# Weight loads of a two-branch spectral filter: +k and -k rows from one DMA queue in turn, in place of two queues side by side

## The chip, the cores and the metric

The kernel runs on one core of one Trainium2 chip. The metric is the device time of one execution in microseconds (us). The core has five engines that work side by side, each with its own instruction queue: TensorE (PE; PEld is its weight load), VectorE (DVE), ScalarE (ACT), GpSimd (POOL) and SyncE (SP). SyncE and GpSimd only issue transfers here. "SPq" in the profile is an issue on SyncE's queue.

## The reference

Two branches, A and B, filter the same input in the frequency domain, and a gate mixes them. Branch B's function is the same as A's.

```python
def _A_ref(x, w_r, w_i):
    B, S, D = x.shape                       # 1, 2048, 1024, bfloat16
    X = rfft2(x.astype(float32), axes=(-2, -1))
    W = w_r + 1j * w_i                      # 2048 x 513 each, bfloat16
    return irfft2(X * W, s=(S, D), axes=(-2, -1)).astype(bfloat16)

x = A_x
g = sigmoid((x * gate_w).sum(-1, keepdims=True))
return g * _A_ref(x, A_w_r, A_w_i) + (1 - g) * _B_ref(x, B_w_r, B_w_i)
```

Only `A_x` is used; both branches share one forward transform.

## The kernel before

The transforms are written as matrix products. A row index of 2048 is split into 128 x 16, a column index is folded into even and odd halves, and constant matrices (FM, DM, S2, KI, DI, RM) carry the cosines and sines. All of x, the transformed x, and both weights lie in on-chip memory: R1 holds x, R4 the transform X, R5 the weight of A, R2 the weight of B. R1 is used again for the inverse result of A (`VR[0]`), and R5 for that of B (`VR[1]`). R2 also holds, before B's weight comes, the gate vector and a row of 2048 numbers made from it, under the keys `gwt` and `zrow`.

The work goes in stages.

1. For 16 slices of x: fold on VectorE (L316), then eight matmuls with FM (L313), then the eviction to R3 on ScalarE. Along the way `gate_row` makes the gate's spectral row, and 16 small matmuls turn it into ZG.
2. The main loop, t from 0 to 20. Step t issues `stage_d(t)` (matmuls with DM, evicted to the buffer Q), `stage_s2(t-1)` (matmuls with S2, evicted to R4 as X), `stage_i1(0, t-5)` (matmuls with KI on the products of A, evicted to R1 as V(0, k)), and at even t one `prod` on VectorE. `prod(b, m)` multiplies X(2m) and X(2m+1) by the weight of branch b: two large multiplications and two smaller combinations, all at L316. At t = 18 comes `prod(1, 0)`, at t = 20 `prod(1, 1)`. At t = 17 stand `x512`, `p512(0)` and `p512(1)`, which treat the last column, number 512, of both weights.
3. A second loop does `stage_i1(1, t)`, the remaining products of B, the gate's mixing rows (`gmix`, L566) and `stage_dinv(0, ...)` with DI.
4. A third loop does `stage_dinv(1, t)` and `s1inv(t-1)`, whose results go out in 16 transfers on SyncE's queue.

The order on each engine is the program's order; nothing is sorted. Class `Sched` works out the waits. Every operation names the keys that it reads and writes. An operation waits for the last writer of each key that it reads; for each key that it writes, it waits for the last writer and for all operations that have read the key since. A transfer counts as done when it has landed. `ev` (L302 on ScalarE, L304 on VectorE) picks the engine of an eviction by estimated loads of these two alone. Matmul results sit in three slots of PSUM in turn (`slot`).

The transfers are issued by `dma` (L319). SyncE's queue holds, in order: x in five pieces with FM behind the first, DM, S2, KI, GS, ID, then the rows of A from `wload(0)`, those of B from `wload(1)` (called at t = 0), DI, RM, two copies of one row (`v512_row`), and the outputs.

A weight's rows are laid out on the partitions so that a frequency k and its mirror -k can be used together. `wload(b)` loops over `ii` (four groups), `c` (real, imaginary) and `pm` (0 for +k rows, 1 for -k rows). Each piece is 16 partitions of 16 rows of 513 numbers, 1,026 bytes a row; the -k rows are read in falling order, and their last group is in two pieces. That makes 8 transfers of +k rows and 10 of -k rows, 4.2 MB for each weight. The +k rows are issued from SyncE, the -k rows from GpSimd. The GpSimd half names `("x", 15)`, the last piece of x, as read. Each half has a key of its own, `("W", b, 0)` and `("W", b, 1)`, and for B both also name `zrow` and `gwt` as written.

The eviction of V(0, 0), in `stage_i1`, is the first write into R1 after x; it names all 16 keys of x as written:

```python
w = [("V", b, kg)]
if kg == 0:
    w += allx if b == 0 else [("W", 0, 0), ("W", 0, 1)]
```

Of the kernel before, what the change touches and what calls it, by code (L numbers as in the profile page):

```python
# [234 lines left out]
def bass_gated_mix__spectral_gfnet__spectral_gfnet__prompt_kernel(  # L235
# [6 lines left out]
    def sb(name, n, dty=BF):  # L242
        t = nc.alloc_sbuf_tensor(name, [128, n], dty)
        pit[id(t)] = n
        return t

    def ap(t, off, dims, p0=0, np_=128):
        return AP(t, p0 * pit[id(t)] + off, [[pit[id(t)], np_]] + [list(d) for d in dims])
# [18 lines left out]
    X5 = sb("X5", 32)  # L267
# [19 lines left out]
    def slot():  # L287
        s = slot_n[0] % nslots[0]
        slot_n[0] += 1
        return s  # L290

    def dve(ns, fns, reads, writes):
        load["dve"] += ns
        return S.op("dve", fns, reads, writes)

    def ev(n, outap, inap, reads, writes, eng=None, bias=0.0):
        ca, cd = 170 + 0.833 * n, 150 + 1.04 * n
        if eng is None:
            eng = "act" if load["act"] + ca <= load["dve"] + cd + bias else "dve"
        load[eng] += ca if eng == "act" else cd  # L300
        if eng == "act":
            S.op("act", lambda e: e.activation(outap, inap, ACT.Copy), reads, writes)  # L302
        else:
            S.op("dve", lambda e: e.tensor_copy(outap, inap), reads, writes)  # L304

    def pslot(s, off, dims, p0=0, np_=128):
        return ap(PS, s * 1024 + off, dims, p0, np_)
# [4 lines left out]
    def mm(o, l, r, start, stop):  # L312
        return lambda e: e.matmul(o, l, r, start=start, stop=stop, skip_group_check=True)  # L313

    def tt(o, a, b, op):
        return lambda e: e.tensor_tensor(out=o, in0=a, in1=b, op=op)  # L316

    def dma(eng, pairs, reads, writes, kind=True):
        S.op(eng, [lambda e, d=d, s=s: e.dma_start(d, s) for d, s in pairs], reads, writes, dma=kind)  # L319
# [19 lines left out]

    def wload(b):  # L340

        both = ([], [])
        T = WR[b]
        P = pit[id(T)]
        for ii in range(4):
            for c in range(2):
                for pm in range(2):
                    src = wsrc[b][c]
                    n = src.shape[-1]
                    prs = both[pm]  # L350

                    def part(r0, step, k0, k1):
                        prs.append((AP(T, (4 * pm + ii) * P + (2 * k0 + c) * NS, [[8 * P, 16], [2 * NS, k1 - k0], [1, n]]),
                                    AP(src.tensor, src.offset + r0 * n, [[128 * n, 16], [step * n, k1 - k0], [1, n]])))
                    if pm == 0:
                        part(16 * ii, 1, 0, 16)
                    elif ii < 3:
                        part(80 + 16 * ii, -1, 0, 16)
                    else:
                        part(127, -1, 1, 16)  # L360
                        part(64, 1, 0, 1)
        dma("sp", both[0], [], [("W", b, 0)] + (["zrow", "gwt"] if b else []))
        dma("pool", both[1], [("x", 15)], [("W", b, 1)] + (["zrow", "gwt"] if b else []))
    wload(0)


# [44 lines left out]
    for n2 in range(16):  # L411
        w = ap(R2, n2 * 128, [[1, 128]], 0, 1)
# [6 lines left out]
    allx = [("x", m) for m in range(16)]  # L419
# [34 lines left out]
    def prod(b, m):  # L454

        T = WR[b]
        x = ap(R4, 2 * m * 1024, [[1024, 2], [512, 2], [1, 512]])
        w = ap(T, 2 * m * 2 * NS, [[2 * NS, 2], [NS, 2], [1, 512]])
        ws = ap(T, 2 * m * 2 * NS + NS, [[2 * NS, 2], [-NS, 2], [1, 512]])
        r = [("X", 2 * m), ("X", 2 * m + 1), ("W", b, 0), ("W", b, 1)]  # L460
        p = PO + m % 2 * 2048
        dve(1230, tt(ap(RING, TO, [[1024, 2], [512, 2], [1, 512]]), x, w, ALU.mult), r, ["t0"])
        dve(1230, tt(ap(RING, TO + 2048, [[1024, 2], [512, 2], [1, 512]]), x, ws, ALU.mult), r, ["t1"])
        for c, op in enumerate((ALU.subtract, ALU.add)):
            t = TO + 2048 * c
            dve(680, tt(ap(RING, p + c * 512, [[1024, 2], [1, 512]]), ap(RING, t, [[1024, 2], [1, 512]]),
                        ap(RING, t + 512, [[1024, 2], [1, 512]]), op), [f"t{c}"], [("P", m % 2, c)])
# [3 lines left out]
    def stage_i1(b, kg):  # L471
        s = slot()
        p = PO + kg // 2 % 2 * 2048 + kg % 2 * 1024
        z = 512 if kg == 0 else 0
        fns = []
        for lb in range(4):
            for c in range(2):
                w = ap(RING, p + c * 512 + lb % 2 * 256 + lb // 2, [[2, 128]])
                fns.append(mm(pslot(s, lb * 256, [[1, 256]]), w, ap(KI, z + c * 256, [[1, 256]]), c == 0, c == 1))
        S.op("pe", fns, [("P", kg // 2 % 2, 0), ("P", kg // 2 % 2, 1), "KI"], [("ps", s)])  # L480
        w = [("V", b, kg)]
        if kg == 0:
            w += allx if b == 0 else [("W", 0, 0), ("W", 0, 1)]
        ev(1024, ap(VR[b], kg * 8, [[128, 128], [1, 8]]), pslot(s, 0, [[8, 128], [1, 8]]), [("ps", s)], w)

    def x512():
# [2 lines left out]
    def p512(b):  # L489
        T, o = WR[b], b * 96  # L490
        x = ap(X5, 0, [[16, 2], [1, 16]])
        w = ap(T, 512, [[NS, 2], [2 * NS, 16]])
        ws = ap(T, NS + 512, [[-NS, 2], [2 * NS, 16]])
        r = ["X5", ("W", b, 0), ("W", b, 1)]
        dve(100, tt(ap(P5, o, [[16, 2], [1, 16]]), x, w, ALU.mult), r, [("p5", b, 0)])
        dve(100, tt(ap(P5, o + 32, [[16, 2], [1, 16]]), x, ws, ALU.mult), r, [("p5", b, 1)])
        for c, op in enumerate((ALU.subtract, ALU.add)):
            dve(100, tt(ap(P5, o + 64 + 16 * c, [[1, 16]]), ap(P5, o + 32 * c, [[1, 16]]),
                        ap(P5, o + 32 * c + 16, [[1, 16]]), op), [("p5", b, c)], [("P5", b, c)])
# [39 lines left out]
    for t in range(16 + 5):  # L539
        if t < 16:  # L540
            stage_d(t)
        if 1 <= t < 17:
            stage_s2(t - 1)
        if t >= 5:
            stage_i1(0, t - 5)
        if t >= 2 and t % 2 == 0:
            prod(t // 18, t // 2 - 1 - t // 18 * 8)
        if t == 0:
            wload(1)
            cload("sp", DI, "DI", 2048)  # L550
            cload("sp", RM, "RM", 2048)
        if t == 17:
            x512()
            p512(0)
            p512(1)
        if t == 19:
            v512(0)
            v512(1)
# [14 lines left out]
    for t in range(16 + LAG):  # L573
        if t < 16:
            stage_i1(1, t)
            if t % 2 == 1 and t // 2 + 2 < 8:
                prod(1, t // 2 + 2)
        if t in (8, 10, 12, 14):
            gmix((t - 8) // 2)
        if t == 15:  # L580
            v512_row(1)
        if t >= LAG:
            stage_dinv(0, t - LAG)
# [64 lines left out]
```

## Time and profile before

| What | Value |
|---|---|
| Median of 2 runs | 181.97 us (180.98 and 182.96) |
| Profiled execution, time | 182.96 us |
| Profiled execution, span of its instructions | 181.1 us |
| TensorE matmuls busy | 129.4 us (71%) |
| VectorE busy | 120.6 us (67%) |
| ScalarE busy | 121.6 us (67%) |
| GpSimd busy | 11.3 us (6%) |
| Bytes moved by DMA | 19.53 MB, mean 108 GB/s |

The profile is of one execution. The span runs from the first instruction to the last; the time of the execution is 1.86 us longer. "Busy" adds up the durations of an engine's instructions; a share of the span says nothing of where the idle time lies. Where lines stand in the text below, a group is named by its line in the kernel, its engine, the operation, and out<-in by the program's tile names without their numbers, so that R is any of R1 to R5.

### The profile page before, as it was taken

To read this page: it belongs to the slowest core of one execution; us is meant where nothing else is said; L and a number is where in the kernel's file an instruction comes from. 1 tells how busy PE (TensorE), PEld (TensorE's weight loads), DVE (VectorE), ACT (ScalarE), POOL (GpSimd) and SP (SyncE) were. 2 spreads that over 40 slices of the span, in tenths; PEclk is the share of its full clock that TensorE was granted. 3 is DMA by queue.
4 is the path that set the end of the run, shared out by engine and by line. 5 is a ranking of instruction groups with operands and counts; after the bars stand their busy time and mean duration, and the time that the engine had idled before them with its cause. 6 is when DMAs were issued, how large, how long until landed. Compare 5 with 4: busy or idle time off the path is not lost.

```text
span 181.1 us, 2542 instructions
## 1 busy us (share of the span) xinstructions
PE 129.4 (71%) x1015; PEld 91.9 (51%) x1024; DVE 120.6 (67%) x193; ACT 121.6 (67%) x132; POOL 11.3 (6%) x24
## 2 busy tenths in 40 slices
PE   0445998889600004999999559999699989998950
PEld 0345463555300003677776337889577757565620
DVE  0799990008950000268998999998693469899994
ACT  2255498399400005689889844899999959987970
POOL 0004700000009100000000000000000000000000
PEclk9999999999975555599999985999999999999997
DMA  6999999999998990000000000000000003334334
GB/s 180 331 423 374 171 224 222 218 165 166 166 243 169 161 144 0 0 5 2 0 0 4 0 0 0 5 0 0 4 0 0 1 4 116 116 138 157 121 114 171
DMA packets 10157, 19.53 MB, mean 108 GB/s; under 512 B 1505, under 2 KB 5793, under 8 KB 9762
## 3 DMA queue, kind: packets, MB, share of 16 engines
q1 hardware_dynamic: 8592, 15.17, 31.6%
q0 software_dynamic: 1408, 4.20, 12.3%
q8 instruction: 8, 0.13, 0.3%
q10 hardware_dynamic: 146, 0.00, 0.0%
q14 instruction: 3, 0.02, 0.0%
HBM read 15.17 MB, written 4.19 MB: 107 GB/s over the span
## 4 chain that ended last, share of the span: by engine, by line
ACT 31%; PE 27%; DMA 17%; DVE 13%; issue 5%; SPq 3%; POOL 2%; POOLq 0%; DVEq 0%; ACTq 0%
PE PS L313 27%; ACT R L302 20%; DMA R<-in_B_w_i_dram 14%; ACT RING L302 8%; DVE RING L316 7%; DMA R<-in_A_x_dram 4%; DVE R L316 3%; SPq L319 3%; DVE RING L304 3%; POOL R L319 2%; ACT GROW L566 1%; ACT L566 1%; ACT V L302 1%; POOLq L213 0%; DVEq L213 0%
## 5 line engine op out<-in xcount | busy, mean ns | idle before, releaser
L302 ACT ACTIVATE R<-PS 128x1024 bf16<-128x1024 f32 (+1 forms) x80 | 75.7, 1039 | 42.8 <-DMA R<-in_B_w_i_dram 22.0
L316 DVE TENSOR_TENSOR RING<-RING 128x512 bf16<-128x512 bf16 (+1 forms) x96 | 44.6, 509 | 22.5 <-PE PS L313 20.3
L316 DVE TENSOR_TENSOR RING<-R 128x2048 bf16<-128x2048 bf16 (+1 forms) x48 | 48.0, 1041 | 14.2 <-DMA R<-in_A_w_i_dram 6.8
L313 PE MATMUL PS<-KI,RING 128*128 128x256 bf16 x256 | 35.9, 291 | 26.4 <-ACT R L302 24.1
L302 ACT ACTIVATE RING<-PS 128x1024 bf16<-128x1024 f32 x40 | 42.8, 1135 | 8.5 <-PE PS L313 7.3
L313 PEld LDWEIGHTS PS<-KI,RING 128*128 128x128 bf16 x256 | 25.3, 104 | 33.7 <-ACT R L302 25.2
L313 PE MATMUL PS<-DI,R 128*128 128x256 bf16 x256 | 32.7, 273 | 1.5 <-DVE RING L304 1.2
L313 PEld LDWEIGHTS PS<-DI,R 128*128 128x128 bf16 x256 | 24.4, 98 | 8.4 <-DVE RING L304 2.2
L313 PE MATMUL PS<-FM,R 128*128 128x128 bf16 x128 | 12.0, 266 | 11.7 <-DVE R L316 11.4
L313 PE MATMUL PS<-RING,S 128*128 128x1 bf16 (+2 forms) x91 | 16.7, 315 | 1.3 <-ACT RING L302 0.8
L313 PE MATMUL PS<-DM,R 128*128 128x256 bf16 x128 | 17.3, 282 | 0.1
L313 PEld LDWEIGHTS PS<-FM,R 128*128 128x128 bf16 x128 | 10.1, 122 | 13.7 <-DVE R L316 12.3
L304 DVE CAST RING<-PS 128x1024 bf16<-128x1024 f32 x8 | 10.0, 1252 | 6.0 <-PE PS L313 6.0
L313 PEld LDWEIGHTS PS<-DM,R 128*128 128x128 bf16 x128 | 12.4, 101 | 2.9 <-ACT RING L302 0.7
L313 PEld LDWEIGHTS PS<-RING,S 128*128 128x128 bf16 x96 | 8.1, 100 | 8.1 <-ACT RING L302 1.4
L316 DVE TENSOR_TENSOR R<-RING 128x1024 bf16<-128x1024 bf16 x16 | 10.4, 688 | 0.3
L313 PE MATMUL PS<-R,FM 128*128 128x512 bf16 x30 | 9.1, 379 | 1.3 <-DVE RING L304 1.3
L313 PE MATMUL PS<-R,G 128*1 128x512 bf16 x32 | 8.8, 423 | 0.7 <-ACT R L302 0.7
L313 PE MATMUL PS<-RING,DM 128*128 128x512 bf16 x30 | 9.1, 379 | 0.1
L304 DVE CAST R<-PS 128x1024 bf16<-128x1024 f32 x4 | 4.9, 1223 | 3.1 <-PE PS L313 3.1
L313 PEld LDWEIGHTS PS<-R,G 128*1 128x1 bf16 x32 | 2.6, 90 | 5.8 <-issue 2.0
L313 PEld LDWEIGHTS PS<-RING,DM 128*128 128x128 bf16 x32 | 3.1, 98 | 3.8
(29 smaller groups left out, 36.0 us busy)
## 6 DMA issues: line engine op xcount, KB each, us to landing
out_dram<-RING SPq DMA_DIRECT2D x16, 256.0 KB, 2.0
R<-in_A_x_dram SPq DMA_DIRECT2D x3, 1024.0 KB, 10.5
R<-in_A_w_r_dram SPq DMA_DIRECT2D x4, 256.5 KB, 16.2
R<-in_A_w_i_dram SPq DMA_DIRECT2D x4, 256.5 KB, 17.8
R<-in_B_w_r_dram SPq DMA_DIRECT2D x4, 256.5 KB, 9.8
R<-in_B_w_i_dram SPq DMA_DIRECT2D x4, 256.5 KB, 10.8
R<-in_A_x_dram SPq DMA_DIRECT2D x2, 512.0 KB, 5.0
R<-in_A_w_r_dram POOLq DMA_DIRECT2D x3, 256.5 KB, 11.2
```

What stands on the lines that cost most here:

```text
L302: S.op("act", lambda e: e.activation(outap, inap, ACT.Copy), reads, writes)
L304: S.op("dve", lambda e: e.tensor_copy(outap, inap), reads, writes)
L313: return lambda e: e.matmul(o, l, r, start=start, stop=stop, skip_group_check=True)
L316: return lambda e: e.tensor_tensor(out=o, in0=a, in1=b, op=op)
L319: S.op(eng, [lambda e, d=d, s=s: e.dma_start(d, s) for d, s in pairs], reads, writes, dma=kind)
L566: S.op("act", lambda e: e.activation(ap(GROW, 0, [[1, 512]]), misc(7, 0, [[1, 512]]), ACT.Sigmoid), ["m7"], ["GROW"])
```

## The change

`wload` collects all pieces of a weight in one list, in the order of its loops: for each group and each of real and imaginary, the +k rows and then the -k rows. One `dma` on SyncE issues the list. It names nothing as read, and one key, `("W", b)`, as written (with `zrow` and `gwt` for B, as before). The users of the weight read that key. GpSimd issues no transfers any more. The order of instructions on TensorE, VectorE and ScalarE stays as it was.

```diff
     def wload(b):
 
-        both = ([], [])
+        prs = []
         T = WR[b]
         P = pit[id(T)]
         for ii in range(4):
...
                     src = wsrc[b][c]
                     n = src.shape[-1]
-                    prs = both[pm]
 
                     def part(r0, step, k0, k1):
...
-        dma("sp", both[0], [], [("W", b, 0)] + (["zrow", "gwt"] if b else []))
-        dma("pool", both[1], [("x", 15)], [("W", b, 1)] + (["zrow", "gwt"] if b else []))
+        dma("sp", prs, [], [("W", b)] + (["zrow", "gwt"] if b else []))
...
-        r = [("X", 2 * m), ("X", 2 * m + 1), ("W", b, 0), ("W", b, 1)]
+        r = [("X", 2 * m), ("X", 2 * m + 1), ("W", b)]
...
-            w += allx if b == 0 else [("W", 0, 0), ("W", 0, 1)]
+            w += allx if b == 0 else [("W", 0)]
...
-        r = ["X5", ("W", b, 0), ("W", b, 1)]
+        r = ["X5", ("W", b)]
```

## The prediction

> **What bounds the kernel now.** I read the waits first, then the timeline around the longest of them, then the transfer rates by stretch, and last the place where the second weight is first used. The table of waits has, per row, who waited on whom, the total in us, how often, and the longest.
>
> ```profile
> POOL R L319 <- DMA R<-in_B_w_i_dram: 32.5, 1, 32.5
> ...
> PE PS L313 <- ACT R L302: 26.0, 8, 22.0
> ACT R L302 <- DMA R<-in_B_w_i_dram: 22.0, 1, 22.0
> ...
> DVE RING L316 <- DMA R<-in_A_w_i_dram: 6.8, 1, 6.8
> ```
>
> One ScalarE instruction waits 22.0 us for the second weight's transfers, and TensorE's longest wait, 22.0 us, is for that instruction. Which one it is, the timeline tells (start, duration, engine, operation, and in brackets the idle time before it with its releaser):
>
> ```profile
> 41.36 2.36 DVE L316 TENSOR_TENSOR RING<-R 128x2048 bf16<-128x2048 bf16 x2 [6.80 <-DMA R<-in_A_w_i_dram]
> ...
> 45.22 1.03 PE L313 MATMUL PS<-KI,RING 128*128 128x256 bf16 x8
> 46.09 1.10 ACT L302 ACTIVATE R<-PS 128x1024 bf16<-128x1024 f32 x1
> ...
> 47.26 1.06 PE L313 MATMUL PS<-RING,S 128*128 128x512 bf16 x6
> ...
> 53.93 0.58 POOL L319 DMA_DIRECT2D R<-in_B_w_r_dram  x1 [32.47 <-DMA R<-in_B_w_i_dram]
> ...
> 69.20 1.02 ACT L302 ACTIVATE R<-PS 128x1024 bf16<-128x1024 f32 x1 [22.01 <-DMA R<-in_B_w_i_dram]
> ...
> 70.28 1.89 PE L313 MATMUL PS<-KI,RING 128*128 128x256 bf16 x8 [21.96 <-ACT R L302]
> ...
> 75.48 1.42 PE L313 MATMUL PS<-KI,RING 128*128 128x256 bf16 x8
> ```
>
> The matmuls at 45.22 are the first `stage_i1(0, 0)`; the activation at 69.20 is its eviction into R1. It does not use the second weight. It waits because it overwrites x (`allx`), and the GpSimd loads are entered as readers of `("x", 15)`: whoever overwrites x waits until both GpSimd loads have landed. The second of them was itself late. It and the SyncE half both list `zrow` and `gwt` as written, so GpSimd held its eight B issues until SyncE's half had landed at 53.65, and its own rows landed at 69.11. From 48.32 to 70.28 TensorE did nothing. It also came back at half clock: i1, d and s2 from 70.28 to 75.48 took 5.20 us, where three stages take about 3.15 elsewhere (1.03 to 1.06 each, as at 45.22 and 47.26); the granted clock in that stretch is 0.50, against 1.00 before the stall.
>
> **Part by part.** *Removed: the read of x15 and the second tile key.* There is now one load per weight, on SyncE, that reads nothing. The eviction of V(0,0) keeps only the wait for TensorE's matmuls. What it can then wait for is the first weight, through the product and i1(0,0).
>
> *Moved: ten issues per weight from GpSimd to SyncE.* Each takes about 0.61 us there (the B rows' issues at 34.98, 35.63 and on), so 6 us per weight. For A they fit where SyncE stood 15.8 us until 34.38, waiting for the gate's matmuls. If the queue holds SyncE back until room is free, the ten wait for 256 KB each at the rate below, 1.6 us, and the last leaves around 35 to 41, still before the queue runs dry. GpSimd's queue has nothing else in it. Behind the B rows on SyncE come DI, RM, the two `v512_row` copies and the outputs, in that order; none of them is wanted before 89 us on the new clock (below).
>
> *The price: one queue instead of two.* In these rows the last number is GB/s.
>
> ```profile
> 18.00:22.00 4.00, 4.00 (x20) 1.78 (x18) 3.93 (x7) 1.94 (x2) 3.47 (x7) 1.00 1.14 169
> 22.00:34.00 12.00, 10.27 (x98) 5.55 (x97) 5.36 (x9) 9.45 (x12) 0.00 (x0) 1.00 1.07 223
> ...
> 36.00:40.00 4.00, 3.25 (x27) 2.17 (x27) 0.00 (x0) 4.00 (x5) 0.00 (x0) 1.00 1.14 165
> ...
> 58.00:66.00 8.00, 0.00 (x0) 0.00 (x0) 0.00 (x0) 0.00 (x0) 1.42 (x3) 0.50 1.04 163
> ```
>
> SyncE's queue alone moves weight rows at 165 to 169 (36 to 40, and 18 to 22, when GpSimd's rows hardly flowed yet), GpSimd's alone 163 (58 to 66), both together 223. In the 8 us from 24 to 32 the two queues stood so (packets, MB, share of the 16 engines' time):
>
> ```profile
> q0 software_dynamic: 416, 1.37, 77.3%
> q1 hardware_dynamic: 417, 0.40, 28.0%
> ```
>
> GpSimd's queue took 171 GB/s, SyncE's only 50, which is why SyncE's last A load, issued at 17.89, landed 23.3 us later, at 41.2. [...]
>
> New landing of A: 4.20 MB at 165 GB/s is 25.5 us. The rate falls from 384 GB/s (16 to 17) over 289 to 173 (18 to 19), so weight rows begin at about 17.5: landed at 43.0. A second way to it: SyncE's half of B, 2.1 MB, followed A at 41.2 and landed at 53.65, so the slowest of the 16 engines needs 12.45 us per half, 24.9 for a whole; from 18 that gives 42.9. The first product starts at 43.0 instead of 41.36, ends 3.57 us later at 46.6, and i1(0,0) starts at 46.6 instead of 45.22: **+1.4 us**. (The product had 0.3 us to spare.) This rests on one thing no row shows: the -k rows, read in falling order, on SyncE's queue. The nearest rows are the same rows on GpSimd's queue (163) and the +k rows on SyncE's (165), so I take 165; the far bounds are 223 (both queues; A at 36.3, no loss) and 50 (SyncE's share beside GpSimd).
>
> *What follows.* i1(0,0) ends at 47.65; ScalarE, free since 47.19, evicts it at 47.7 instead of 69.20. TensorE runs d(6) and s2(5) to 49.8 and goes straight on with i1(0,1): its bank is free at 48.7. So the 21.96 us of idle time go: **-22.0**. The clock has no reason to fall in a gap of 1.4 us, so the next three stages take 3.15 instead of 5.20: **-2.05**. The following pair, i1(0,2) and d(8), took 2.34 to 77.82 and should take 2.1: **-0.2**. Sum: -22.8 us; the stage at 77.82 starts at 55.0.
>
> What could take it back behind that? VectorE worked ahead during the stall: it did the product at 49.88 while the others stood. Now product 1 runs 46.6 to 50.2, a cast to 51.4, product 2 to 55.0. Product 2 is wanted by i1(0,4), two rounds of 2.65 after i1(0,2) at 52.9, so at 58; cover 3 us. The cast of d(8) then begins at 55.0, and 77.81 less 22.8 is 55.0. The rounds from 77.82 on are TensorE's (5.3 us for two, VectorE 4.9), unchanged. That products don't slow down beside transfers is seen in their durations: 2.36 for the pair at 45.14, with the queues full, and 2.36 at 79.76, with none.
>
> *The wait that is added.* B's first user now waits for B itself; before, ScalarE's stall had covered it. It is the small product `p512(1)` on VectorE:
>
> ```profile
> 104.58 0.34 DVE L316 TENSOR_TENSOR P<-X,R 128x32 bf16<-128x32 bf16 x2
> ```
>
> Behind it VectorE has all products of B, and TensorE's i1(1, ...) waits for those. On the new clock it comes at 81.8. B follows A in the same queue: 43.0 + 25.5 = 68.5, so 13 us are to spare. DI and RM (1 MB; 254 GB/s from 50 to 54) land at 72.6; DI is wanted at 115.68 - 22.8 = 92.9, and SyncE's row copy, at 112.09 before, at 89.3.
>
> The profiled execution has a span of 181.1 and a time of 182.96, the median of the two runs is 181.97. Span 158.3; time 160.2 by the profiled run, 159.2 by the median. I give 159.7.
>
> **Rivals.** (1) *The -k rows are somewhat slow on SyncE's queue*, or the slowest DMA engine falls further behind in a longer run of rows. At 130 GB/s a weight takes 32.3 us: A at 49.8, 6.8 later, B at 82.1, just in time. Time 166.5. For it: no row has -k rows on this queue, and SyncE's queue was pushed to 50 once. Against it: 163 for the same rows elsewhere.
>
> (2) *They are very slow, and B becomes the bound.* From `p512(1)` to the end the old kernel needs 76.5 us of span, so this turns slower once B lands after 104.6, that is when a weight takes over 43.5 us. The +k half takes 12.7 of that, so the -k half would have to flow under 2.1 MB / 30.8 us = 68 GB/s. At 50 it takes 42, a weight 54.7, B lands at 126.9; time 126.9 + 76.5 + 1.9 = 205. For it only the shared stretch; against it that this is the share beside another queue, which is gone.
>
> (3) *The eviction is still held by B's load through another key.* Then it would go when all B rows have landed, 68.5 instead of 69.11: time 182.4, no change. Against it: the only other keys on that eviction are the 16 x loads, long landed, and V(0,0) itself.
>
> **How the numbers follow.** Forecast 0.85, rival 1 0.07, rival 2 0.05, rival 3 0.03. The forecast's own range: down to 158 if A lands as early as before, 157 with the lower run; up to 163 if a weight takes 29 us (145 GB/s), 164.5 with the runs' spread and a clock that dips in the short gap. That holds 0.8 with a little to spare, so the range is 157 to 164.5. About 2%, 3.6 us, can be told from no change here: faster 0.92, same 0.03, slower 0.05.
>
> **What would show it.** Right: no row of ScalarE waiting on B; the first eviction of i1 near 47.7; TensorE's longest idle time in the first 100 us under 8; granted clock 1.00 from 43 to 80; rate near 165 from 18 to 68; VectorE's wait for A about 8.4 us instead of 6.8; no wait for B at `p512(1)`. Wrong: A's landing past 46, a VectorE wait for B near 82, or a stall at the first eviction that ends with B.

## The result and the profile after

| | Before | After |
|---|---|---|
| Median | 181.97 us (2 runs, 180.98 and 182.96) | 157.88 us (2 runs, 157.44 and 158.32) |
| Ratio, 95% interval | | 0.868 (0.845 to 0.890) |
| Profiled execution: time, span | 182.96, 181.1 | 157.44, 155.9 |

The changed kernel is faster by 13%. The forecast was 159.7 us (157 to 164.5) and faster.

The table of waits of the changed kernel begins like this (who waited on whom, total us, times, longest):

```profile
ACT R L302 <- PE PS L313: 17.8, 15, 5.4
PEld PS L313 <- DVE R L316: 14.5, 7, 7.3
PE PS L313 <- DVE R L316: 13.1, 6, 7.3
DVE RING L316 <- ACT R L302: 8.4, 5, 6.4
```

No engine waits for a weight any more, neither ScalarE for B nor VectorE for A. The 6.4 us that VectorE stands ahead of the first product are now put down to ScalarE, that is to the eviction of X. The same stretch in the timeline (start, duration, engine, operation, idle time before it and its releaser):

```profile
40.94 2.36 DVE L316 TENSOR_TENSOR RING<-R 128x2048 bf16<-128x2048 bf16 x2 [6.41 <-ACT R L302]
...
45.18 1.03 PE L313 MATMUL PS<-KI,RING 128*128 128x256 bf16 x8
...
46.06 2.03 ACT L302 ACTIVATE R<-PS 128x1024 bf16<-128x1024 f32 x2
...
48.15 1.03 PE L313 MATMUL PS<-KI,RING 128*128 128x256 bf16 x8
...
51.16 1.03 PE L313 MATMUL PS<-KI,RING 128*128 128x256 bf16 x8
...
53.12 0.84 PE L313 MATMUL PS<-RING,S 128*128 128x512 bf16 x5
```

The two ScalarE instructions from 46.06 are an eviction of X and, right behind it at about 47.1, the eviction of V(0,0) that stood until 69.20 before. The second i1 starts at 48.15 instead of 70.28. The rates (last number, GB/s; the number two ahead of it is the granted clock of TensorE):

```profile
43.00:80.00 37.00, 33.94 (x274) 24.50 (x277) 34.02 (x42) 33.39 (x34) 0.00 (x0) 1.00 0.42 100
...
18.00:34.00 16.00, 13.06 (x119) 7.30 (x117) 9.44 (x16) 11.84 (x14) 0.00 (x0) 1.00 1.13 215
34.00:50.00 16.00, 14.59 (x125) 9.98 (x124) 8.60 (x11) 14.67 (x14) 0.00 (x0) 1.00 1.12 248
```

The clock stays at 1.00 where it had been at 0.50. And one queue alone moves the weight rows at 215 and 248 GB/s, where SyncE's queue alone had moved 165 to 169 before. That was not forecast, and half of the experiments are about it.

### The profile page after: what moved, and what is told of

The parts are those of the page before. It is cut to its first block, busy times and chain, and to the rows that moved or that the text cites. A ratio compares the mean times of both kernels' runs of the same rounds, so it can differ in the third digit from the quotient of the medians.

```text
span 155.9 us, 2541 instructions
## 1 busy us (share of the span) xinstructions
PE 124.6 (80%) x1015; PEld 89.8 (58%) x1024; DVE 120.4 (77%) x193; ACT 121.6 (78%) x132; POOL 0.2 (0%) x4
## 3 DMA queue, kind: packets, MB, share of 16 engines
q1 hardware_dynamic: 13008, 19.37, 45.1%
## 4 chain that ended last, share of the span: by engine, by line
ACT 39%; PE 27%; DVE 21%; issue 6%; DMA 4%; SPq 1%; DVEq 0%
PE PS L313 27%; ACT R L302 22%; ACT RING L302 14%; DVE RING L316 11%; DVE R L316 6%; DMA R<-in_A_x_dram 4%; DVE RING L304 3%; ACT GROW L564 1%; ACT L564 1%; ACT V L302 1%; SPq L319 1%; DVEq L213 0%
## 5 line engine op out<-in xcount | busy, mean ns | idle before, releaser
L316 DVE TENSOR_TENSOR RING<-RING 128x512 bf16<-128x512 bf16 (+1 forms) x96 | 44.6, 509 | 2.5 <-ACT RING L302 1.4
L313 PE MATMUL PS<-KI,RING 128*128 128x256 bf16 x256 | 33.8, 280 | 4.3 <-DVE RING L316 2.2
L313 PEld LDWEIGHTS PS<-KI,RING 128*128 128x128 bf16 x256 | 24.2, 100 | 10.6 <-ACT R L302 2.8
L313 PE MATMUL PS<-RING,S 128*128 128x1 bf16 (+2 forms) x91 | 15.8, 304 | 1.3 <-ACT RING L302 1.1
L313 PE MATMUL PS<-DM,R 128*128 128x256 bf16 x128 | 16.5, 273 | 0.3 <-ACT RING L302 0.2
L313 PEld LDWEIGHTS PS<-DM,R 128*128 128x128 bf16 x128 | 11.8, 97 | 3.0 <-ACT RING L302 1.1
L313 PE MATMUL PS<-R,G 128*1 128x512 bf16 x32 | 7.5, 378 | 0.7 <-ACT R L302 0.7
```

## Experiments

Two questions were put. First, did the time come from the dropped reader's entry, or from the new queue and order of the rows? Second, why did one queue not run at 165 GB/s? Ratios are to the kernel before on the same chip, with 95% intervals.

**Only the entry dropped** (e2). Two queues and both start times stay as before.

```diff
-        dma("pool", both[1], [("x", 15)], [("W", b, 1)] + ...
+        dma("pool", both[1], [] if b else [("x", 15)], [("W", b, 1)] + ...
```

> The kernel before with one edit: GpSimd's half of B is no longer entered as a reader of x. Two queues and the late start of B's second half stay. If the 22 us are the eviction of V(0,0) waiting for a load that it does not need: that wait is gone, A lands at 41.4 as before, B's second half lands at about 69, before its use at about 80, and the time is 157.5 to 159. Rival: the gain comes from the transfers' new order and queue; then the time stays within a few us of 182.

158.70 us, ratio 0.876 (0.870 to 0.881). GpSimd still held B's second half back until 53.9, and no engine waited for it:

```profile
POOL R L319 <- DMA R<-in_B_w_i_dram: 31.9, 1, 31.9
ACT R L302 <- PE PS L313: 20.2, 14, 5.9
...
DVE RING L316 <- ACT R L302: 8.4, 5, 6.4
```

The long row of GpSimd is still there, but no compute engine waits behind it. Dropping one entry in a list of keys gives the whole gain.

**The same beside the changed kernel** (e11 and e12), with more runs on one chip:

> The changed kernel again, beside the others on one chip: 157.9.

> The kernel of the run e2_no_read again (two queues, B not entered as a reader of x), beside the changed kernel on one chip. What is left between the two is what queue and order are worth by themselves. A landed before X was ready in both, so 0 to 0.8 us; if A's landing at 41.4 still counted, 1 us or more.

Changed kernel 158.39 us, ratio 0.872 (0.869 to 0.876); two queues without the entry 157.98 us, ratio 0.870 (0.867 to 0.874). The intervals overlap: queue and order by themselves are worth nothing that these runs can tell. One premise of the expectation did not hold. In the profile of e12 the first product did wait for A:

```profile
41.32 2.36 DVE L316 TENSOR_TENSOR RING<-R 128x2048 bf16<-128x2048 bf16 x2 [7.03 <-DMA R<-in_A_w_i_dram]
...
44.86 2.36 DVE L316 TENSOR_TENSOR RING<-R 128x2048 bf16<-128x2048 bf16 x2
```

VectorE stood 7.03 us there, against 6.41 us for X in e11, both after the same instruction (the one that writes ZG), so A came some 0.6 us after X. The second product, at 44.86, follows without a wait, where VectorE stood 0.60 us ahead of it in e11. So a landing of A 0.6 us after X cost nothing here.

**The entry put back into the changed kernel** (e4).

```diff
-        dma("sp", prs, [], [("W", b)] + ...
+        dma("sp", prs, [("x", 15)] if b else [], [("W", b)] + ...
```

> The changed kernel with the load of B entered as a reader of x again; queue and order of the rows stay. If the entry is the cause, the first eviction of i1(0, ...) waits until all of B has landed, at about 57 instead of 47.1; TensorE stands for about 9.5 us and runs on at half clock for three stages (2 us more): 168 to 170. Rival (the new queue and order made the gain): 158.

172.45 us, ratio 0.949 (0.939 to 0.959). The eviction waits again, for all of B:

```profile
46.40 1.10 ACT L302 ACTIVATE R<-PS 128x1024 bf16<-128x1024 f32 x1
60.48 1.02 ACT L302 ACTIVATE R<-PS 128x1024 bf16<-128x1024 f32 x1 [12.98 <-DMA R<-in_B_w_i_dram]
```

The mechanism came as expected, 13.0 us of it instead of 9.5. In this execution B moved at 210 to 228 GB/s, not 250, and landed 3.5 us later than I had reckoned.

**The other false wait taken away instead** (e3): the entry stays, but GpSimd's half of B no longer names `zrow` and `gwt`.

```diff
-        dma("pool", both[1], [("x", 15)], [("W", b, 1)] + (["zrow", "gwt"] if b else []))
+        dma("pool", both[1], [("x", 15)] + ([("W", 0, 0)] if b else []), [("W", b, 1)])
```

> The kernel before with the other of its two waits taken away: GpSimd's half of B no longer names zrow and gwt as written (it writes none of those places), and starts when SyncE's half of A has landed, at about 41, instead of at 53.9. It is still entered as a reader of x, so the first eviction of i1(0, ...) still waits for it. If that reader's entry makes the wait and the key only its length: B's second half lands at about 41.3 + 15 = 56, the eviction goes there instead of at 69.2, and the time falls by some 12 to 13 us, to about 169. Rival (the late second half as such costs the time): 158, as with the entry removed.

177.96 us, ratio 0.980 (0.972 to 0.987); expected was 169. The eviction did go when the half landed, but at 66.13, not 56:

```profile
66.13 1.02 ACT L302 ACTIVATE R<-PS 128x1024 bf16<-128x1024 f32 x1 [18.15 <-DMA R<-in_B_w_i_dram]
```

GpSimd issued from 40.59 on, yet no packet of its queue is in the trace up to 47, and then it shared the engines. From 58 to 62, when SyncE's queue had rows of DI and RM as well (queue, packets, MB, share of the engines' time):

```profile
q1 hardware_dynamic: 147, 0.48, 54.0%
q0 software_dynamic: 146, 0.40, 49.6%
```

The two queues moved equally many packets in these 4 us, 147 and 146, so the bytes of each went with the size of its packets. In the stretch shown in the prediction it was 416 to 417 packets, 1.37 to 0.40 MB. The 15 us that I gave that half are what it took in the profile before, alone or beside little else. Here its first packets came over 6 us after the first issue, against 1 to 2 us there (issue at 53.93, first packets between 55 and 56). That is about 5 of the missing 10 us; the rest fits the sharing, but no run tests it alone.

The five kernels that differ in this wait line up:

| Kernel | V(0,0)'s eviction starts, us | Median, us |
|---|---|---|
| before | 69.20 | 181.97 |
| e3, key removed | 66.13 | 177.96 |
| e4, entry put back | 60.48 | 172.45 |
| e2, entry removed | about 47.5 | 158.70 |
| after | about 47.1 | 157.88 |

Each us of the eviction's start is about one us of the time. The runs were made on more than one chip (beside e3 and e4 the kernel before took 181.52). The step from e4 to e2, 13 us for 13.8, has the half clock in it as well (granted 0.50 from 56 to 62 in e4, 1.00 in e2).

**All +k rows first on the one queue** (e1).

```diff
-        for ii in range(4):
-            for c in range(2):
-                for pm in range(2):
+        for pm in range(2):
+            for ii in range(4):
+                for c in range(2):
```

> The changed kernel with one edit: on SyncE's single queue all +k rows of a weight come first and then all -k rows. Theory P (place): what sets the rate is which partitions the transfers in flight write to. The +k rows go to partitions 0 to 3 of each eight, the -k rows to 4 to 7; with one kind alone in flight the rate is about 165 GB/s, as in the kernel before, so A lands at about 43 us, B at about 68, and the time is 1.4 us over the changed kernel, 159.3. Theory S (source): the rate depends on rows being read from two regions, rising and falling; it gives the same 165 here. Theory Q (queue): one queue is as quick as two, and the kernel before was slow for another reason; then the rate is 215 to 250, A lands before 41, and the time is 157.9.

Ratio 0.896 (0.890 to 0.902), 162.5 us (median of six executions, 162.0 to 165.0). One queue is back at the rate of 165, so that rate goes with the order of the rows, not with the queue:

```profile
18.00:34.00 16.00, 13.90 (x124) 7.43 (x121) 9.25 (x15) 11.54 (x14) 0.00 (x0) 1.00 1.13 169
34.00:40.00 6.00, 5.24 (x48) 3.88 (x46) 0.17 (x1) 4.87 (x5) 0.00 (x0) 1.00 1.14 166
```

A landed at 45.3 and not 43. By then these rates had moved about 4.6 MB, 0.4 MB more than A has: rows of B had already moved while the last rows of A were still under way. The first product started 4.4 us later than in the changed kernel, and the time is about 4 us longer where 1.4 was expected. Theories P and S both said 165; Q falls.

A late A can also cost more than the delay. The execution profiled here took 164.99 us, and in it TensorE came back at half clock:

```profile
48.96 1.86 PE L313 MATMUL PS<-KI,RING 128*128 128x256 bf16 x8 [3.85 <-issue]
```

The granted clock was 0.76 on average from 46 to 50 and 0.59 from 50 to 56. In e8 (below), after a gap of 3.1 us, it was 0.75 and 0.88 in these stretches; in e6 (below), after 2.7 us, it stayed at 1.00.

**Place or source** (e5 and e6). In e5 the places alternate and the sources do not; in e6 the sources alternate and the places come in halves.

```diff
# e5, in the order of the changed kernel: every -k piece reads the +k piece's rows
-                    elif ii < 3:
...
+                    else:
+                        part(16 * ii, 1, 0, 16)
# e6, in the order of e1: rows chosen by c, places by pm
-                    if pm == 0:
+                    if c == 0:
```

> The changed kernel, with the -k pieces copied from the same source rows as the +k pieces, rising (so the -k half of the weights has other values). The places written still alternate. Theory P: the rate stays at 215 in A and about 250 in B. Theory S: it falls to about 165, and A lands at about 43. [...]

> The converse: the sources alternate between +k and -k rows, but the places are filled in halves, first all partitions 0 to 3 of each eight, then all 4 to 7 (so some rows land in another row's place, and the values differ). Theory P: about 165 GB/s throughout, A lands at about 43. Theory S: 215 to 250 as in the changed kernel, A lands before 41.

e5, places alternating (158.09 us, one run):

```profile
18.00:34.00 16.00, 14.30 (x106) 7.07 (x104) 9.11 (x15) 11.31 (x14) 0.00 (x0) 1.00 1.13 208
34.00:40.00 6.00, 5.08 (x53) 3.80 (x55) 0.17 (x1) 4.38 (x5) 0.00 (x0) 1.00 1.13 220
```

e6, sources alternating (161.22 us, one run; A landed at 45.1 and not 43):

```profile
18.00:34.00 16.00, 14.68 (x108) 7.44 (x105) 9.24 (x15) 10.94 (x14) 0.00 (x0) 1.00 1.14 169
34.00:40.00 6.00, 4.71 (x50) 3.56 (x52) 0.17 (x1) 4.38 (x5) 0.00 (x0) 1.00 1.13 165
```

In these two runs the rate followed the places written, whether the source rows were the same or different: 208 and 220 GB/s with places alternating, 169 and 165 with places in halves. Theory S falls.

**Which places** (e8): the order of e1, but `ii` innermost, so that consecutive transfers change partition within the lower four of each eight.

```diff
+        for pm in range(2):
+            for c in range(2):
+                for ii in range(4):
```

> One queue, all +k rows first as in the run e1_plus_first, but consecutive transfers now go to partitions 0, 1, 2, 3 of each eight in turn instead of twice to each. If any change of partition between consecutive transfers were enough, the rate would be 208 or more; if only the step between the lower and the upper four of each eight helps, it stays at 165 to 175, and A lands at about 45 as in that run. [...]

161.86 us (one run), and A landed at 44.6:

```profile
18.00:34.00 16.00, 13.79 (x120) 7.43 (x119) 9.39 (x16) 11.54 (x14) 0.00 (x0) 1.00 1.13 169
34.00:40.00 6.00, 5.25 (x52) 3.92 (x50) 0.17 (x1) 4.72 (x5) 0.00 (x0) 1.00 1.13 165
```

A change of partition within the four was not enough: 169 and 165 GB/s, as in e1. The runs with changes between the lower and the upper four of each eight moved 208 and 220 (e5), 215 and 248 (the changed kernel). What lies behind this no run shows.

**A shorter turn** (e7): pieces of 8 rows, +k and -k in turn, 36 transfers a weight.

```diff
-                for pm in range(2):
+                for pm, kh in ((0, 0), (1, 0), (0, 1), (1, 1)):
...
+                    k0, k1 = 8 * kh, 8 * kh + 8
```

> The changed kernel with every piece cut in two, 8 rows each, +k and -k in turn: 36 transfers a weight instead of 18. Theory P, finer: the places written mix better when the turn is shorter, so A moves at about 250 GB/s from the start instead of 215 and lands at 35 instead of some 39. The first product waits for the X rows until 40.9 in any case, so the time stays at 157.9. Rival: twice as many issues, 0.6 us each, hold SyncE up: the issues of B then end near 57 instead of 48, B lands later, but before its use at 80; also 157.9. If the turn's length does not matter, A's rate stays at 215.

158.5 us, ratio 0.873 (0.867 to 0.880): no gain, as expected. The rate from 18 to 34 was 240. That doesn't show that the turn's length made it: the changed kernel's own second profile (e11) has 240 there as well, and 198 for B, where the first had 215 and 248. With both kinds in flight the rate moved between about 200 and 250 from one execution to the next. The two profiles with short pieces are at the upper end from 18 to 34 (240, and 247 in e10), but what sets the rate stays open.

**What bounds the kernel now** (e9 and e10). If the first product waits for X, X should come earlier. The gate's last sums stand ahead of the main loop; they are moved into it.

```diff
+        if n2 == 12:
+            gate_row(2)
...
-    gate_row(3)
...
+        if t == 1:
+            gate_row(3, 7, "dve")      # bank 7, evicted by VectorE
...
-        if t == 0:
-            wload(1)
+        if t == 2:
+            gate_sum()                 # the 16 small matmuls and ZG
+            wload(1)
```

> The changed kernel with the gate's sums moved out of the way of the main loop's start: the third gate row is made one pair of slices earlier, the fourth behind the second stage_d (in another PSUM bank, evicted by VectorE), and the 16 small matmuls and the load of B that waits for them come at step 2. In the changed kernel stage_d(0) starts at 34.24 us though its inputs are there at 30.3, and the first product waits for X until 40.9. Now X should be there at about 37.5. A lands at about 39.3 in the changed kernel, so the first product starts at about 39.5: 1 to 1.5 us faster, 156.5. Rival (the start of the loop doesn't set the end, or the moved matmuls cost as much later): 157.9.

> The same, with the pieces of 8 rows of the run e7_half_pieces, in which A moved at 240 GB/s and lands at about 35. Then X is the last to come, at about 37.5, and the gain is 2.5 to 3.5 us: 155. If A's landing were no bound in the run before, both runs give the same time.

e9: 156.20 us, ratio 0.863 (0.858 to 0.867), faster than the changed kernel beside it (0.872, 0.869 to 0.876). It is the fastest version here. The start of the main stretch in e9:

```profile
39.33 2.36 DVE L316 TENSOR_TENSOR RING<-R 128x2048 bf16<-128x2048 bf16 x2 [3.48 <-ACT R L302]
```

X comes at 39.3, 2 us earlier than in the changed kernel's run beside it (41.36) and not the 3.5 hoped for: the moved gate row stands on TensorE ahead of the first `stage_s2`. It is X still, not A, that the product waits for. So e10, with its shorter turns, should bring nothing more, and didn't: 156.83 us, 0.863 (0.860 to 0.867). My 155 for it was wrong.

## Why the prediction was right, and where it was not

**The mechanism and the main term held.** The false reader's entry was the stall, shown by taking it away alone (e2) and by putting it back alone (e4). Forecast -22.0 us for TensorE's idle time; the second i1 moved by 70.28 - 48.15 = 22.1.

**The half clock held.** Forecast -2.05; the three stages took 51.16 - 48.15 = 3.01 us against 5.20, so -2.2. That a gap of 1.4 us leaves the clock alone was an estimate of mine; in the profile before, TensorE's gaps of 1.93 us ahead of 10.85 and 1.78 us ahead of 14.82 left it at 1.00. The next pair took 53.12 - 51.16 = 1.96 against 2.34, -0.4 for a forecast of -0.2.

**The step that failed is the price of one queue.** Forecast +1.4 us, from "4.20 MB at 165 GB/s", A at 43.0. Measured: the first i1 at 45.18 against 45.22, so 0. A's last pieces were issued by 30.2 and took about 10 us to land, by about 40, before X was there at 40.9. The term was mis-sized because 165 GB/s was read as the rate of *a queue*. In the profile before, each queue alone also meant one kind of row alone, and both queues together meant both kinds. The rows could not tell queue from kind, and I did not name that as a choice. For the same reason 223 against 165 looked like the worth of a second queue. With both kinds in one queue the rate was 215 and 248; with one kind at a time in one queue it was 169 and 166 (e1, up to 40). Without the 1.4 us the forecast would have been 158.3; 157.88 came.

A slip without consequence: GpSimd had ten issues of B, as the part on the moved issues says, and not the eight named in the part on the stall.

**The sum.** Forecast -22.8 up to the stage that began at 77.82; measured 53.12, so -24.7. The difference of 1.9 is the 1.4 of that term, 0.3 of the two clock terms and 0.1 of the idle time. The span fell by 25.2; the other 0.5 lies behind.

**B's wait.** No wait at `p512(1)`, as forecast, and with more room than reckoned: the last rows of B were issued by 47.9, and the transfers behind them (DI and RM) landed at 57.6 and 58.8, while the small product came at 79.87. Rival 1 (slow -k rows) and rival 2 (very slow ones) have nothing for them: e1, with its -k rows alone in the second half, shows 166 to 178 throughout. Rival 3 is excluded by the waits.

**The signs named.** The first eviction (47.7 forecast, 47.1), the clock, and TensorE's longest idle time (7.3 us) came as said. "Near 165 from 18 to 68" and "VectorE's wait for A about 8.4" were the wrong ones, both from the failed term.

**What the range was worth.** With A at 45.3, as in e1, the time is 162.5, still inside it. The first number was right within 1.2% because the failed term is small, not because it was known.

## What to carry to other kernels

Where a wait tracker takes "read" and "written" keys, a key named only to delay a transfer makes that transfer a reader or a writer, and whoever uses the place next waits until it has landed: look for the instruction that waits for data it does not use. Before giving a rate to a queue, ask what else differed between the rows that it was read from, above all which partitions they wrote (here 165 to 175 GB/s against about 195 to 250, from one queue). A transfer that lands before its user is ready can be made faster without any gain (e7, e10); find what comes last at that point first.

## What was not expected of the hardware

- Rows of 1,026 bytes written only to partitions 8q to 8q+3, or only to 8q+4 to 8q+7, moved at 163 to 175 GB/s, from either queue, in the stretches of six kernels that held little else (before, e1, e2, e3, e6, e8). With both groups in flight it was about 195 to 250, from one queue or two.
- Two queues with work moved equally many packets (417 and 416 in one stretch, 147 and 146 in another). In the first the queue with the larger packets got 171 GB/s and the other 50.
- GpSimd's rows began to flow over 6 us after their first issue while SyncE's queue still had many rows to move (e3: issue at 40.59, no packet of its queue up to 47). With little left on SyncE's queue they flowed after 1 to 2 us (before: issue at 53.93, first packets between 55 and 56). No run tests the cause.
